# Second feed-forward product as seven half products, operands in the attentions' buffers

## Chip, core and metric

The kernel runs on one core of a Trainium2 chip. The metric is the device time of one execution in microseconds (us). Three executions were timed and one more was profiled.

## What is computed

Three layers follow each other, for a batch of 4 sequences of 448 positions and 768 channels:

```python
# 1: causal attention, 12 heads of 64
x = softmax(causal(q @ k.T / 8)) @ v
# 2: four one-head attentions (experts) on x; each position takes its best two
logits = x @ w_gate
out = sum(gate[e] * (softmax(causal((x @ wq[e]) @ (x @ wk[e]).T / 8)) @ (x @ wv[e])) @ wo[e] for e in range(4))
# 3: feed-forward with a gate from a convolution over positions (3 taps)
h = relu(out @ w_in)                      # 768 -> 1024
y = h * sigmoid(conv(h, conv_w))
result = y @ w_out                        # 1024 -> 768: the product that is changed
```

`w_in`, `conv_w` and `w_out` arrive as 64-bit floats.

## The kernel before

Every product is made from numbers split in two: a high part (`hi`) that TensorE takes without loss, and the rest (`lo`). Three matmuls (`PASSES`) stand for one exact product: hi by hi, hi by lo, lo by hi. Splitting a tile therefore takes two elementwise instructions, a copy for hi and a subtraction for lo. ScalarE is called ACT, VectorE DVE, GpSimd POOL and SyncE SP, as in the profile.

**Stages.** For each batch `b` there are six attention jobs of two heads (`A`, from layer 1), the projections of layer 2 (`proj_qk`, `proj_v`) and two jobs of layer 2's attentions (`M`). Layer 2's `wo` and layer 3's `w_in` are folded into one matrix `wp` beforehand (`fold_all`). `ffn_batch` makes, for each batch, eight chunks of 128 feed-forward channels: six matmuls with 448 moving columns (L1188), then relu, convolution, tanh, the gate product (L1219), and the split of the result `g` (L1223, L1226). `ffn_out(b, n)` makes 128 output channels of a batch: for each of the eight chunks three matmuls of 448 moving columns against `wout` (L1251), 24 in all, then one copy out of PSUM and one store of 224 KB.

**Weights.** `wout_convert` takes `w_out` in 12 pieces of 512 columns: a load, a conversion from 64-bit floats (one ACT and four DVE instructions, `from_f64`), hi on ACT (L1105), lo on POOL (L1108), and a store into device memory. When the attentions of layer 1 are over, six loads of 1 MB bring the split weights back (`wout_load`).

**Order.** Nothing is scheduled at run time. All tasks are numbered as they are added, and `ORDER` is a packed list, written out beforehand by a planner, which gives the order of the tasks and, where a task may run on several engines (`either`), the engine. Each engine executes its tasks in that order. The planner's costs are in the code; for a matmul it reckons

```python
def mm(n, k=1):
    return k * max(n / 2.2, 96.0)
```

**Buffers.** Tiles come from rings (`RINGS`), PSUM banks from `BANKS`. The operands `g` of two batches have room at once: eight tiles in a pool of their own and eight in the ring of `xT`. The rings `P` and `PT` hold the attentions' probabilities and their transposes, `skM` the operands of layer 2's attentions. The part of the order behind layer 1's last attention mixes the projections and the `M` jobs of batch 3 with `ffn_batch` and `ffn_out` of batches 0 to 2: `M[3, 0]` ends its product with the values before the first `ffn_out` of batch 0 is over, `M[3, 1]` in the midst of batch 1's.

Of the kernel before, what the change touches and what calls it, by code (L numbers as in the profile page):

```python
# [14 lines left out]
I64 = mybir.dt.int64  # L15
# [25 lines left out]
    "ST9h^C~Li|-e3QWv&q@z9CD60Z#k!|e^Dqjh~B6#*GKEQa-E!pHpw|?pFArM%P&w@s2^Al*dI9Ooc(%rr?zuI{-GX1!)Q~dqZ5*QJ0G*2vOd>8"
    "WA)eN>OQcpS?Ic?+%AXZg}SA>mAd!!=k>SsC^=XsuDj%fJCmJyv>9zjU)IBQ)H*De$YpRj+_}2%YwmU4aE9gMb@@78-I)BD{E_^L{IUE&rxz{b"
    "66E7GlQlCng_`*q6<5!-a7#6dHLEpLxsR)>8|UUbr|M$pFn79hwsW*|uJilO&6=$mXWed1r6yA6sq5$FxjF7Ecc{)-w@|lHx6pZ5b5e6zb6Qib"
    "JFY9q*W|Y~0F^)mcyub4Dxqf4IW)){Mh|h5bxH1`e2NQGljtIs%Y%3@Z%h8NQ^)i2LcDGH7<vM2;vv*Y+H>wS?Fns-wn5vWEphEUD(_?6`?^nc"
    "=XIBLW~!6wqeiG{YCrW)-T*blyRAd93G7e2$LIq3Gw*^oOdX>>qEgv!xo@~1Xg{MD&<|?X<=fmT>Qn0L&L#9JI?LNYm(deEGkuVrr#tAsb?$WT"
    "bq>?#X>Vx*ylwPz+Ck?pEG}Ej{-*vJ^#!#eSFj`W6>f!l!hK17MSa`3NIRen@lx~+>T%~4cb~g2@1q~f&$u_-hrEyIL-Z8=wDTX{9S_4N@@IJS"
    "yeB+t7p-f7hwtL@mw78Zi2siIp1Mc<MCEiHQ+0e3|Cn|`{Yt~o?`Rjaubn=AmJf9)y2AWl1dD=K0+?UnAMoAWP2MP7+hyku@RR&u{utjwpQY#d"
    "fPf<q3qZje!4>tEN}$u|0F6MS)3`J-jVkyXUF6Tvm*@)G?}BZCrRyo5OIOkn`Z@oSe=gt(A>pL}5n2Hq%}jIBe6$EnOoxSK-Vy(ruMi-D9bTH&"
    "N6XRv?PT)b&|lGC(6{In`U!oTzE3};8-;)n6jFtk=o|E7eu=-v-{4;h973-U4V<F?7J$G<!6!jUxFp;ZmW3X{B7cj&&A*~w(_Mn7z#>Qs`UHc5"
    "A;GvHFQ^F5g#VR)m2V5b6W$YMgi+y$a8x)cEC`Fj8#$)oK<MuB0%70*jliHW%#1LD3akiuz!#x|kpkEZJCFrt1f&K=1Fzvocq2rM7$TxbDv~f1"  # L50
    "3=cyBz`%cKTZ|pXA!Ay2#Q>Q%j3<IQ0b7)0Xc<{Xj&aNw5siy<4W<TP1C?oS2sbE2W|2dLh<qX};|E|;ByBiv0ALWlZ1})H02K3-!C^wokf^^Q"
    "*YJ>WpYfRSh*4ma7&D?k*KhD&@H_ZDJOv~hij1KKDm)9!0bCe@#~RY2KGAakfpelIV4`8VVE|ZU!0;NQAo>Uc3Y`K}Y%s1H=0yu4lVY}ENyJs?"
    "nJ%V^X<_=9X=WcY%p7D6Gw%cAz-RaZ{tB-&EH+RTp{`<sT>&XzMXD>?mFpVr@+ww<apnZm2!|A#igU%K!U4Z%*lc*)uqLV~b{h^G-T<4TEzz#X"
    "3*UpwiXW9vlmqa!Vov!&nSm>!L(vxS2ar-^6%Q5L3bgV-@uA_k;Yfj3<`j<<N1`(kP03N}l@(<O9)TxeKwN;&mFk9{x_(u@Qod1MD#u`j@<2%t"
    "11h>0RB^=;u~KXjBjSHVYR$j!6g=AXsB1`3gg*c?ig`r|ey2PDmK9RvF~Cus0ha((wV-&SxCR#CRamUDD4oim)&Gi$T?7eDVwQv@UZq14&|ol5"
    "u}>Tkr^Wr^LGhUQNO`SPs1Vh#_{S~+hKkve>_|RH4kgDDql$ykYb+X<CZg<D=9H7-s3xlNtDbkIlrySX)r`0xo)?$I%i<03ieg3VQl(XWszKG2"
    "WL!0&I+bKJ_cTjgt6dviZ@b=ifl{jUMuL+5)wQYG67PyD;zRL?_+0!&TvpwP(NIaX2}vXz=~>sF>at5Ax#>FUl6lY`B1DCFkQ7ouddLDfAdiGC"
    "(MtT#k}3+NpnFgb8dBjsBg#=_Qj(SAB=@1b<i2D?Gp2#0d8JFb1?@r=NG~0SN}46j_nL>28O^?GMFo4lQE#h?s$<n-iArjbPC_$K0h)(qHAT&t"
    "3ZpJa`qU-KqGU}1sy8GXnxdoxEkdi1vI%K=t2u<6P2Q#zjZYeqrlohP2~Ad-Zpt<pn|3sV(qZXv(^nN;Em3pS3iS!}o%$5IufBvz>P>a1NvAfd"
    "|LpohInXrP^dI#j^<(u@^`7Qbv!q^8SJVgUGxZmBS-q{!Hyx=FkICckOgAkw{m5Kw8kaiN9(B5LS6k8Mr8jDHBfhcNlx_5SW*TQ3i;d44!|IX7"  # L60
    "vBpoD&zi5ATMfF2&_rwcrTJy^tL8V&1C29UZWGj0(9Ub0HZeT^LIvrvbWXY|r8Z79vKtp0R~y%wwwl(PcAB=N2htts2Wh2A+Nf+aH`*JIqz_sj"
    "wmxdzXxwi+Xu?W-vVK`umXj?=*QMIVaoMaaFPoD28pDkx?Rhh|1!*z1oJlXGPz&5LB)e?BZU$Pw7HZ4;#*dBf8c!Op8h>wo-+b11(+Frzn$DU&"
    "HZx?OnoBK9Et@Te+7oS2mXzT&&t*$8q6{OulX7KZnNo(xDlKO%<(7k%?UpYsW|>_^*F0|BY&~yvw0K)&m}JXJ%Vkr@^Gfzc_Fh(&aWs&I@9Aqn"
    "8!NIC*_G@@b|$N|E^F7c=h|q?z6_|(cz$Yq*7~A#pyg%jQOixsWoucxp)I$fTN$kftykI`EgHcaVa!O&WD5bIBO^vGB0-dh4*4E4gmIg`H6fVk"
# [53 lines left out]
class Program:  # L118
# [146 lines left out]
def attn_moe_ffn_kernel(  # L265
# [352 lines left out]
    def head(j, h, moe):  # L618
# [87 lines left out]
        for i in range(NQ - 1, -1, -1):  # L706
# [4 lines left out]
            elif i:  # L711
# [5 lines left out]
                if not first:  # L717
                    first = j.taken = [t]
# [666 lines left out]
```

## Time and profile before

| | |
|---|---|
| median of three executions | 503.1 us (501.62 to 504.71) |
| profiled execution, its own time | 503.03 us |
| its span in the trace | 501.2 us |
| granted TensorE clock, mean | 0.996 |
| TensorE busy (matmuls) | 487.5 us |
| DVE, ACT, POOL busy | 369.0, 349.8, 261.9 us |

The span runs from the first instruction to the last; 1.8 us of the profiled time lie around it. A matmul's busy time includes its way through the array, and matmuls overlap, so that TensorE shows as busy also across short gaps. What one matmul costs in a row of many is the time of the row divided by their number.

### The profile page before, as it was taken

To read this page: it belongs to the slowest core of one execution; us is meant where nothing else is said; L and a number is where in the kernel's file an instruction comes from. 1 tells how busy PE (TensorE), PEld (TensorE's weight loads), DVE (VectorE), ACT (ScalarE), POOL (GpSimd) and SP (SyncE) were. 2 spreads that over 40 slices of the span, in tenths; PEclk is the share of its full clock that TensorE was granted. 3 is DMA by queue.
4 is the path that set the end of the run, shared out by engine and by line. 5 is a ranking of instruction groups with operands and counts; after the bars stand their busy time and mean duration, and the time that the engine had idled before them with its cause. 6 is when DMAs were issued, how large, how long until landed. Compare 5 with 4: busy or idle time off the path is not lost.

```text
span 501.2 us, 9905 instructions
## 1 busy us (share of the span) xinstructions
PE 487.5 (97%) x3202; PEld 419.7 (84%) x3202; DVE 369.0 (74%) x1110; ACT 349.8 (70%) x970; POOL 261.9 (52%) x388
## 2 busy tenths in 40 slices
PE   8788999999999999999999999999999999999997
PEld 6656878988888898888988788898999989999996
DVE  4999999988899686987789984487587556374300
ACT  5989999998889768886888893386566554344201
POOL 1856879978879777998788944162022002000000
PEclk9999999999999999999999999999999999999999
DMA  8857468996793767665688615838220112101011
GB/s 216 211 164 186 128 179 225 232 250 192 203 242 106 178 173 214 142 176 136 202 204 237 151 57 168 272 148 213 88 90 0 56 37 80 51 16 58 37 38 73
DMA packets 29171, 73.03 MB, mean 146 GB/s; under 512 B 4160, under 2 KB 11072, under 8 KB 28352
## 3 DMA queue, kind: packets, MB, share of 16 engines
q1 hardware_dynamic: 29040, 72.18, 51.8%
q8 instruction: 25, 0.41, 0.4%
q10 hardware_dynamic: 80, 0.23, 0.2%
q14 instruction: 26, 0.21, 0.1%
HBM read 50.50 MB, written 13.63 MB: 128 GB/s over the span
## 4 chain that ended last, share of the span: by engine, by line
PE 74%; DVE 11%; POOL 5%; DMA 4%; issue 2%; ACT 1%; SPq 0%; POOLq 0%; DVEq 0%; ACTq 0%
PE bank L1251 23%; PE bank L952 9%; PE bank L690 9%; PE bank L760 9%; PE bank L637 9%; PE bank L1188 8%; PE bank L998 4%; DMA nat<-in_qk_dram 4%; DVE P_A L650 3%; PE bank L881 3%; POOL sk_A L340 2%; DVE PT_A L337 1%; POOL P_M L333 1%; POOL P_A L333 1%; DMA cwraw<-in_conv_w_dram 1%
## 5 line engine op out<-in xcount | busy, mean ns | idle before, releaser
L1251 PE MATMUL bank<-g,wout 128*128 128x448 f32 x576 | 123.2, 367 | 0.0
L1251 PEld LDWEIGHTS bank<-g,wout 128*128 128x128 f32 x576 | 107.4, 188 | 8.8
L659 ACT ACTIVATE P_A<-P_A,nm_A 112x448 f32<-112x448 f32 (+3 forms) x192 | 99.4, 521 | 15.7 <-DVE nm_A L650 10.4
L340 POOL TENSOR_TENSOR sk_A<-nat,sk_A 64x448 fp32r<-64x448 f32 (+1 forms) x77 | 90.3, 1172 | 9.7 <-ACT sk_A L331 3.9
L650 DVE CUSTOM_DVE_ANT_0 P_A<-bank,mask 112x448 f32<-112x448 f32 (+3 forms) x192 | 80.0, 440 | 10.8 <-PE bank L595 6.3
L637 PE MATMUL bank<-sk_A 128*112 128x112 f32 (+3 forms) x352 | 66.4, 312 | 3.5 <-DVE nm_A L650 2.9
L952 PE MATMUL bank<-xT,wqk 128*128 128x448 f32 x288 | 68.7, 374 | 0.6 <-DVE sk_M L968 0.4
L690 PE MATMUL bank<-ident,P_A 112*112 112x112 f32 x480 | 61.7, 264 | 3.3 <-DVE xT L792 1.4
L333 POOL TENSOR_SCALAR P_A<-P_A,r_A 112x336 f32<-112x336 f32 (+3 forms) x97 | 49.9, 526 | 25.7 <-DVE r_A L670 9.2
L637 PEld LDWEIGHTS bank<-sk_A 128*112 128x112 f32 x352 | 48.8, 176 | 10.1 <-DVE nm_A L650 4.5
L690 PEld LDWEIGHTS bank<-ident,P_A 112*112 112x112 f32 x480 | 49.8, 135 | 8.0 <-DVE xT L792 1.6
L952 PEld LDWEIGHTS bank<-xT,wqk 128*128 128x128 f32 x288 | 51.2, 188 | 4.1 <-DVE sk_M L968 0.5
L1209 DVE SCALAR_TENSOR_TENSOR bank<-h,cw,bank 128x448 f32<-128x448 f32 x64 | 43.5, 687 | 14.8 <-ACT bank L1207 11.6
L760 PE MATMUL bank<-PT_A,v 112*64 112x448 f32 (+3 forms) x384 | 50.4, 406 | 0.1
L760 PEld LDWEIGHTS bank<-PT_A,v 112*64 112x64 f32 x384 | 26.2, 137 | 23.6 <-issue 12.3
L331 ACT ACTIVATE P_A<-P_A,r_A 112x448 f32<-112x448 f32 (+3 forms) x87 | 42.3, 517 | 4.6 <-DVE r_A L670 4.3
L1188 PE MATMUL bank<-ocs,wp 128*128 128x448 f32 x192 | 43.5, 367 | 0.0
L998 PE MATMUL bank<-wvg,xT 128*112 128x260 f32 x288 | 41.2, 287 | 0.2 <-DVE wm L434 0.2
L333 POOL TENSOR_SCALAR sk_A<-nat 128x896 fp32r<-128x896 f32 x35 | 33.0, 941 | 12.6 <-DMA nat<-in_qk_dram 11.6
L1188 PEld LDWEIGHTS bank<-ocs,wp 128*128 128x128 f32 x192 | 35.7, 188 | 3.0
L659 ACT ACTIVATE P_M<-P_M,nm_M 112x224 f32<-112x224 f32 (+3 forms) x64 | 33.3, 522 | 6.8 <-DVE nm_M L650 5.3
L331 ACT ACTIVATE PT_A<-bank 112x336 f32<-112x336 f32 (+1 forms) x75 | 33.9, 472 | 5.2 <-PE bank L690 5.0
(105 smaller groups left out, 820.2 us busy)
## 6 DMA issues: line engine op xcount, KB each, us to landing
nat<-in_qk_dram SPq DMA_DIRECT2D x88, 224.0 KB, 4.0
wraw<-in_w_in_dram SPq DMA_DIRECT2D x12, 512.0 KB, 5.5
woraw<-in_w_out_dram SPq DMA_DIRECT2D x12, 512.0 KB, 5.1
wo<-wohl SPq DMA_DIRECT2D x12, 512.0 KB, 4.1
wout<-wo SPq DMA_DIRECT2D x6, 1024.0 KB, 10.0
v<-in_v_dram SPq DMA_DIRECT2D x24, 224.0 KB, 4.5
out_dram<-osb SPq DMA_DIRECT2D x24, 224.0 KB, 1.9
sk_M<-sk_M SPq DMA_DIRECT2D x16, 224.0 KB, 4.2
```

Source lines behind the costliest of these rows:

```text
L331: nc.scalar.activation(dst, src, AF.Copy, scale=scale)
L333: nc.gpsimd.tensor_scalar(dst, src, scale, 1.0 if scale2 is None else scale2, ALU.mult, ALU.mult)
L340: (nc.gpsimd if e == "POOL" else nc.vector).tensor_tensor(dst, a, b, op)
L637: nc.tensor.matmul(sp[:CP], t[:, j.o[h], m * CP : (m + 1) * CP], t[:, j.o[h] + k, :w], start=(k == 2), stop=(k == 1),)
L650: nc.vector.tensor_tensor_reduce(rows(i), st["s", i][:CP, :w], mask[:, S - w :], -SCALE, 3.0e38, ALU.add, ALU.min, st["nm"][:, i : i + 1],)
L659: nc.scalar.activation(rows(i), rows(i), AF.Exp, bias=st["nm"][:, i : i + 1], scale=-1.0, accum_out=st["sm"][:, i, 0:1],)
L690: nc.tensor.transpose(pt[:CP, o : o + CP], rows(i)[:, kt * CP : (kt + 1) * CP], ident[:CP, :CP])
L760: nc.tensor.matmul(st["ov"][h * D : (h + 1) * D, kt * CP : S], j.v[:, kt, h, :], j.PT[h][:, col_base[kt] : col_base[kt] + S - kt * CP], st ...
L952: nc.tensor.matmul(st["ps"][:, :S], proj["wqk"][:, a, cc, w, p * P : (p + 1) * P], xT[b, cc][:, b2, :], start=(cc == 0 and (a, b2) == PASS ...
L998: nc.tensor.matmul(st[i][:CP, :VW], xT[b, cc][:, a, i * CP : (i + 1) * CP], proj["wvg"][:, b2, cc, :], start=(cc == 0 and (a, b2) == PASSE ...
L1188: nc.tensor.matmul(st["ps", c][:, :S], wp[:, a, ec, c * P : (c + 1) * P], st["oc", ec][:, b2], start=(ec == 0 and (a, b2) == PASSES[0]), s ...
L1251: nc.tensor.matmul(st["ps"][:, :S], ffn["wout", n][:, a, c], gs[c][:, b2], start=(c == 0 and (a, b2) == PASSES[0]), stop=(c == NFC - 1 and ...
```

## The change

`ffn_out(b)` computes a batch's product of 768 by 1024 and 1024 by 448 as a two by two block product with seven multiplications in place of eight (Strassen's scheme in Winograd's form). The weight blocks are 384 by 512, the operand blocks 512 by 224. So there are seven products (`PRODUCTS`), each of three groups of 128 rows (`HO`), each of four chunks (`HC`), each of three passes: 252 matmuls of 224 moving columns a batch in place of 144 of 448.

- Four sums of weight blocks are needed. `wout_convert(m, q)` now converts blocks in pairs and adds and subtracts them (24 instructions of 256 columns), splits seven blocks in place of four, and stores 24 pieces, 10.5 MB in place of 6 MB (`wset_d`, in runs of 1 KB). Seven loads of 1.5 MB bring the sets back.
- Four sums of operand blocks are needed. `chunk_pair` makes, of two chunks, three sums (`t13`, `t2`, `t4`) and splits seven blocks, in four pieces. `mul` writes its result into SBUF in place of PSUM; the factor 0.5 has moved into relu.
- The seven products are summed up in `ffn_sum`, eight instructions of 224 columns for each group of rows, 96 in all, in place of 24 copies of 448. The stores are 32, of one or two quarter blocks.
- The pool `g` is gone. `unit_space` lends out 22 tiles of the rings `xT`, `skM`, `vm`, `PT` and `P`, when the attentions are through with them: 4 for `g` and the sums (`w`), 18 for split operands (`u`). A batch needs 14 of the 18, and 2 for its input.
- `ORDER` is new. Read out against the numbering of the tasks, it differs in this: before layer 1's attentions are over, POOL has 8 copies and 7 subtractions of `q` and `k` less and 3 scalings of probabilities more; ACT has 6 of the copies, 15 evictions of transposes and 4 scalings more; DVE has 7 of the subtractions and 2 of the copies more, 15 evictions and 7 scalings less. Of the weights' copies to hi, 7 are on ACT and 17 on DVE (12 on ACT before), of their subtractions 16 on POOL and 8 on DVE (12 on POOL before), of their sums 20 on POOL and 4 on DVE. Of the operands' sums 27 are on POOL and 21 on DVE, of their splits' copies 31 on ACT, 18 on POOL, 15 on DVE, and of their subtractions 38 on POOL and 26 on DVE. The 24 pieces of converted weights are 6 of 256 columns and 18 of 512. Of the operands' 16 pairs of chunks each has one sum of 448 columns (9 on POOL, 7 on DVE) and two of 224, three splits of 448 columns (17 subtractions and 11 copies on DVE) and one of 224. Both `M` jobs of batch 3 now come directly behind that batch's projections, and end before the second product of batch 0 is well begun; eight `ffn_batch` chunks stand between their steps.

```diff
-    BANKS = dict(s=(0, 1, 4), t=(2, 3, 5), v=(4, 5), m=(6, 7), h=(6, 7, 0, 2), o=(5, 3, 1))
+    BANKS = dict(
+        s=(0, 1, 4), t=(2, 3, 5), v=(4, 5), m=(6, 7), h=(6, 7, 0, 2), o=(5, 3, 1, 4),
+        w=(102, 103, 104, 105), u=(100, 101, *range(106, 122)),
+    )
...
+    PRODUCTS = ((0, "b11"), (1, "b21"), (2, "t2"), (4, "t3"), (5, "t1"), (3, "b22"), (6, "t4"))
...
+        a22 = parts(lambda: vals[1]()[:, 1:2], 1, 6, [vals[1, "t"]])
+        s1 = combine(at(1, 1), at(1, 0), at(1, 1), ALU.add, a22)
+        up = parts(lambda: vals[0](), 2, 0, [vals[0, "t"]])
+        s3 = combine(at(1, 0), at(0, 0), at(1, 0), ALU.subtract, s1 + [vals[0, "t"]])
+        parts(lambda: vals[1](), 2, 4, s3, wms[1:])
+        s2 = combine(at(0, 0), at(1, 1), at(0, 0), ALU.subtract, s3 + up)
+        s4 = combine(at(0, 1), at(0, 1), at(0, 0), ALU.subtract, s2)
+        parts(lambda: vals[0](), 2, 2, s4, wms[:1])
...
+        give([10, 11, 12], of_sk, [t for j in M.values() for t in j.taken], [Buf("skM")])
+        give([13], of_vm, [t for j in M.values() for t in j.vready], [Buf("vm")])
...
+            t = give([14 + k], of_pt, [j.first_tr for j in every] + [t], [Buf("PT")])
...
-                nc.vector.scalar_tensor_tensor(y, y, 1.0, st[c][:, 1 : S + 1], ALU.add, ALU.mult)
+                nc.vector.scalar_tensor_tensor(
+                    g()[:, k], st["ps", c][:, :S], 1.0, st[c][:, 1 : S + 1], ALU.add, ALU.mult
+                )
...
+        t = [add(either("tadd", b, of_two(S)), 0, t13, muls, take=[tb], free=[gb])]
+        t13_done = t
+        t = [add(either("tadd", b, of_two(HS)), 0, t2, t, free=[gb])]
+        t24_done = [add(either("tadd", b, of_two(HS)), 0, t4, t, free=[gb])]
...
+            th = add(either("ghi", b, of_one(n)), 0, hi, dep + after, take=take, free=[buf])
+            tl = add(either("glo", b, of_two(n)), 0, lo, [th], free=[buf])
...
-                    nc.tensor.matmul(
-                        st["ps"][:, :S],
-                        ffn["wout", n][:, a, c],
-                        gs[c][:, b2],
-                        start=(c == 0 and (a, b2) == PASSES[0]),
-                        stop=(c == NFC - 1 and (a, b2) == PASSES[2]),
...
+                            nc.tensor.matmul(
+                                ps(pb)[:, :HS],
+                                wset[s][:, a, m, c2 * P : (c2 + 1) * P],
+                                u[:, b2, o : o + HS],
+                                start=(c2 == 0 and (a, b2) == PASSES[0]),
+                                stop=(c2 == HC - 1 and (a, b2) == PASSES[2]),
+                            )
...
+    SUMS = (
+        (("s", None),),
+        (("c11", "s"),),
+        (("u", "s"),),
+        (("s", "u"),),
+        (("c22", "s"), ("u", "u")),
+        (("c12", "u"),),
+        (("c21", "s"),),
+    )
...
+            if src:
+                nc.vector.tensor_tensor(w, acc, st[src, m], ALU.add)
+            else:
+                copy(e, w, acc)
...
+    for n, (s, _) in enumerate(PRODUCTS):
+        wset_load(s, [ta] if n < 4 else [tg], "wa" if n < 4 else "wb")
     for b in range(B):
-        ffn_batch(b, cwt, [ta, tg] if b % 2 else [ta])
+        ffn_batch(b, cwt, [ta])
     for b in range(B):
-        for n in range(NCC):
-            ffn_out(b, n)
+        ffn_out(b)
```

## Rows read from the trace of the kernel before

**Rows 1.** The page, busy time, share of the span and instructions by engine.

```profile
PE 487.5 (97%) x3202; PEld 419.7 (84%) x3202; DVE 369.0 (74%) x1110; ACT 349.8 (70%) x970; POOL 261.9 (52%) x388
```

**Rows 2.** Busy time in three stretches: PE, PEld, DVE, ACT, POOL, clock, DMA, GB/s.

```profile
50.00:100.00 50.00, 49.45 (x382) 41.65 (x383) 48.76 (x166) 47.72 (x145) 43.12 (x52) 1.00 0.73 190
100.00:300.00 200.00, 198.28 (x1490) 169.22 (x1489) 172.20 (x589) 167.16 (x500) 161.79 (x222) 1.00 0.67 180
350.00:450.00 100.00, 100.00 (x518) 90.52 (x515) 60.87 (x115) 54.20 (x112) 10.90 (x33) 1.00 0.16 52
```

**Rows 3.** Chain that ended last, shares by line, of 75 to 300 and 300 to 502.

```profile
by line: PE bank L690 16.3%; PE bank L637 15.9%; PE bank L952 14.7%; PE bank L760 14.4%; PE bank L881 7.0%; PE bank L998 5.7%; POOL sk_A L340 4.5%; DMA nat<-in_qk_dram 3.3%; POOL P_M L333 2.8%; issue 2.3%; POOL P_A L333 1.8%; DVE P_A L650 1
...
by line: PE bank L1251 58.2%; PE bank L1188 19.4%; PE bank L952 5.7%; PE bank L760 5.0%; PE bank L998 4.4%; PE bank L690 2.9%; PE bank L637 2.2%; ACT osb L331 0.3%; issue 0.0%; ACTq L331 0.0%
```

**Rows 4.** The same chain in order of time: start, length, what, number.

```profile
107.53 1.44 PE bank L881 x12
...
319.76 1.22 PE bank L1188 x6
...
411.14 2.04 PE bank L760 x16
...
461.70 35.88 PE bank L1251 x177
```

**Rows 5.** Groups by line and form: the changed product, weight loads of 128 and 112 columns.

```profile
L1251 PE MATMUL bank<-g,wout 128*128 128x448 f32 x576 | 123.2, 367 | 0.0
L1251 PEld LDWEIGHTS bank<-g,wout 128*128 128x128 f32 x576 | 107.4, 188 | 8.8
...
L637 PEld LDWEIGHTS bank<-sk_A 128*112 128x112 f32 x352 | 48.8, 176 | 10.1 <-DVE nm_A L650 4.5 <-DVE xT L792 0.7 <-issue 0.3
```

**Rows 6.** Timeline of weight loads, windows at 8.4, 6.5 and 77.9: start, length, number.

```profile
8.18 0.52 PEld L1320 LDWEIGHTS bank<-ident 128*128 128x128 f32 x4 [0.48 <-issue]
...
6.52 0.30 PEld L1320 LDWEIGHTS bank<-ident 128*128 128x128 f32 x2 [0.67 <-issue]
...
77.84 0.28 PEld L637 LDWEIGHTS bank<-sk_A 128*112 128x112 f32 x2
```

**Rows 7.** Groups by line and form: elementwise work like what is added or moved.

```profile
L1108 POOL TENSOR_TENSOR wohl<-wm,wohl 128x512 fp32r<-128x512 f32 x12 | 15.4, 1289 | 3.4 <-ACT wohl L1105 2.4 <-POOL sk_A L340 0.9
...
L1105 ACT ACTIVATE wohl<-wm 128x512 fp32r<-128x512 f32 x12 | 7.5, 625 | 2.3 <-DVE wm L434 2.3
...
L340 POOL TENSOR_TENSOR sk_A<-nat,sk_A 64x448 fp32r<-64x448 f32 x42 | 50.0, 1191 | 5.4 <-ACT sk_A L331 1.4 <-POOL P_A L333 0.8
...
L333 POOL TENSOR_SCALAR sk_A<-nat 128x896 fp32r<-128x896 f32 x35 | 33.0, 941 | 12.6 <-DMA nat<-in_qk_dram 11.6 <-PE bank L637 0.6
...
L331 ACT ACTIVATE sk_A<-nat 128x896 fp32r<-128x896 f32 x9 | 8.5, 948 | 0.5 <-DMA nat<-in_qk_dram 0.5
...
L331 ACT ACTIVATE PT_A<-bank 112x336 f32<-112x336 f32 x52 | 22.7, 443 | 3.9 <-PE bank L690 3.9
...
L340 DVE TENSOR_TENSOR sk_A<-nat,sk_A 64x448 fp32r<-64x448 f32 x2 | 1.2, 622 | 0.1
...
L340 DVE TENSOR_TENSOR sk_A<-nat,sk_A 128x448 fp32r<-128x448 f32 x9 | 7.7, 851 | 0.7 <-ACT sk_A L331 0.7
...
L1209 DVE SCALAR_TENSOR_TENSOR bank<-h,cw,bank 128x448 f32<-128x448 f32 x64 | 43.5, 687 | 14.8 <-ACT bank L1207 11.6 <-POOL ocs L1163 1.9 <-issue 0.5
...
L1219 DVE SCALAR_TENSOR_TENSOR bank<-bank,h 128x448 f32<-128x448 f32 x32 | 19.9, 628 | 7.9 <-ACT bank L1215 7.6
...
L650 DVE CUSTOM_DVE_ANT_0 P_A<-bank,mask 112x224 f32<-112x224 f32 x48 | 18.2, 382 | 0.8 <-PE bank L595 0.5
```

**Rows 8.** DMA issues: number, KB each, median us from issue to landing.

```profile
wo<-wohl SPq DMA_DIRECT2D x12, 512.0 KB, 4.1
...
wout<-wo SPq DMA_DIRECT2D x6, 1024.0 KB, 10.0
```

More of the change, by code (lines that the diff above doesn't have):

```diff
@@ L1 @@
 from contextlib import ExitStack
+from functools import partial
 import base64
@@ L393, in attn_moe_ffn_kernel, with from_f64 @@
     open_pool("w", "right")
-    def from_f64(raw, raw_buf, load, shape, n, need=(), take=()):
+    def from_f64(raw, raw_buf, load, shape, n, need=(), take=(), own=None):
         st = {}
@@ L434, in flush @@
             nc.vector.scalar_tensor_tensor(m, m, 2.0**-30, view(st["ps"]), ALU.is_ge, ALU.mult)
-        ts = add("ACT", act_sb(n) + 35, square, [load], take=[sq], free=[raw_buf])
-        t = add("DVE", dve(n), bits, [load, *need], take=[mb, *take])
+        ts = add("ACT", act_sb(n) + 35, square, [load, *need], take=own[0] if own else [sq], free=[raw_buf])
+        t = add("DVE", dve(n), bits, [ts], take=[mb, *take])
         t = add("DVE", dve(n), top, [t])
@@ L446, in mk @@
         j.kind, j.b, j.p = kind, b, p
+        j.began = []
         return j
@@ L1180, in ffn_batch, with chunk_pair, g, tt @@
-        for c in range(NFC):
+        his[b] = []
+        for c2 in range(HC):
+            chunk_pair(b, c2, cwt, need, st, obs, oc, od)
+    def chunk_pair(b, c2, cwt, need, st, obs, oc, od):
+        gb, tb = Buf("w"), Buf("w")
+        def g():
+            return unit(gb)
+        def tt():
+            return unit(tb).rearrange("p a (k n) -> p (a k) n", k=2)
+        muls = []
+        earlier = pairs[-2] if len(pairs) > 1 else []
+        for k in range(2):
+            c = c2 + HC * k
@@ new lines, in chunk_pair, with t13, t2, t4 @@
+            muls.append(add("DVE", dve(S), mul, [t] + muls + earlier, take=[] if k else [gb], free=[hb, mb]))
+        def t13(e):
+            both = g().rearrange("p a n -> p (a n)")[:, :S].rearrange("p (a n) -> p a n", a=2)
+            two(e, tt()[:, 0:2], g()[:, :, HS:], both, ALU.subtract)
+        def t2(e):
+            two(e, tt()[:, 2], g()[:, 1, HS:], tt()[:, 0], ALU.subtract)
+        def t4(e):
+            two(e, tt()[:, 3], g()[:, 1, :HS], tt()[:, 2], ALU.subtract)
+        t = [add(either("tadd", b, of_two(S)), 0, t13, muls, take=[tb], free=[gb])]
@@ new lines, in ffn_out, with part, go @@
+    def ffn_out(b):
+        st = {}
+        tmp = {(k, m): Buf("tmp") for k in ("s", "u") for m in range(HO)}
+        obuf = {}
+        for step, (s, name) in enumerate(PRODUCTS):
+            for m in range(HO):
+                pb = Buf("o")
+                t = None
+                def part(c2, s=s, name=name, m=m, pb=pb):
+                    def go():
+                        ub, o, _ = operands[b, c2, name]
+                        u = unit(ub)
+                        for a, b2 in PASSES:
+                            nc.tensor.matmul(
[4 more added lines that the diff above has]
+                                stop=(c2 == HC - 1 and (a, b2) == PASSES[2]),
+                            )
+                    return go
+                for c2 in range(HC):
+                    ub, _, dep = operands[b, c2, name]
+                    t = add(
+                        "PE", mm(HS, 3), part(c2), dep + wset_done[s] + [t],
+                        take=[] if c2 else [pb], free=[ub],
+                    )
+                for dst, src in SUMS[step]:
+                    ffn_sum(b, m, st, tmp, obuf, t, pb, dst, src)
```

454 lines of the change are left out of this document (285 added, 169 removed).

## The prediction

> **What bounds the kernel now.** I read the page first, then the stretches, then the chain in shares, then the chain in order of time, and last the groups of the changed lines. The page shows TensorE busy 97% of the span and every other engine at 74% or less [rows 1]. Busy is a share of overlapping matmuls, so the chain decides. It splits the run in two. From 75 to 300 us matmuls have 74% of the chain; a fifth lies on POOL, DVE and ACT, 3.3% on a wait for a load [rows 3]. There those three are busy 162 to 172 of 200 us [rows 2]: a stage in which TensorE leads, with little room beside it. From 300 us on the matmul lines have 98% of the chain, L1251 alone 58% [rows 3], while DVE and ACT are busy 61 and 54 of 100 us and POOL 11 [rows 2]. So the change takes matmul time from the stage that consists of it, puts splitting work into the half-empty engines beside it, and weight sums into the full stage ahead.
>
> **The change, part by part.** The working is against the profiled execution, 503.03 us, which is the median of 503.1 within 0.1; its span is 501.2.
>
> *The product itself.* Before: 35.88 us for 177 matmuls in a row [rows 4] is 0.2027 us for 448 columns, and 576 of them [rows 5] cost 116.8 us, all on the chain. After: 7 products x 3 groups x 4 chunks x 3 passes x 4 batches are 1008 matmuls of 224 columns. The planner prices one at 224 / 2.2, or 0.102 us. No row shows 128 stationary columns with 224 moving ones. What streaming would cost follows from two rows: half of 0.2027 is 0.101, and 1.44 us for 12 matmuls of 256 columns [rows 4], 0.120 each, scaled to 224 gives 0.105; I take 0.103. But each matmul brings its own weight load, 576 for 576 [rows 5]. A load of 128 columns lasts 0.188 us and one of 112 lasts 0.176 [rows 5], so part of it goes with the columns. Four loads of 128 columns in a row take 0.52 us; less the 0.19 of the last one, three steps take 0.33, which is 0.110 each [rows 6]. The pair that begins a burst shows the same, 0.30 less 0.19 [rows 6], and a pair of 112 columns about 0.10 [rows 6]. With 448 columns such a load hides behind the streaming (0.110 under 0.203), with 256 as well (under 0.120); with 224 it doesn't (0.110 over 0.103). I take 0.110 as nearest, since it is the step of just this load: 1008 x 0.110 = 110.9, a gain of 5.9 us, where the planner's price would give 14.0. The ends are 0.101 (101.8, a gain of 15.0) and the row of 256 columns, 0.120 (121.0, a loss of 4.2).
>
> The Trainium skill says in TensorE: Matmul & The Clock Gate, section LDWEIGHTS (loading the stationary operand), that a load takes its columns divided by 1.2 ns, however many rows it has. That speaks against halves: 106.7 ns for 128 columns, by which the product would cost 107.6 us, a gain of 9.2. The step in the rows is 3 ns longer, and I stay with the rows. The same page, section Back-to-back issue gap, gives columns / 2.4 + 2.5 ns for one matmul behind another, 95.8 ns for 224 columns, an estimated 96.6 us and a gain of 20.2; for 448 it gives 189.2, and the trace, with 202.7, doesn't agree.
>
> *Weight sums and the new order, ahead of 300 us.* The conversions from 64 bits stay (12 pieces). Priced by rows 7, with 256 columns at half of 512 and a scaling like an eviction: POOL loses 8 copies (0.94) and 7 subtractions (1.19), gains 3 scalings (0.44), and has 11 subtractions of 512 columns (1.29) and 25 subtractions or sums of 256 (0.6) for 12 of 512: +0.5 us. ACT gains 6 copies (0.95), 15 evictions (0.44), 4 scalings, and loses 3.7 us of weight copies (0.62): +10.4. DVE gains 7 subtractions (0.62), 2 copies, 8 weight subtractions (0.85 for 448 columns), 17 weight copies, which no row shows (0.3 to 0.6 for 512, I take 0.5), and 4 sums, and loses 15 evictions and 7 scalings: +13.4. That is 24 us on three engines. They are busy 501 of 3 x 200 us [rows 2], hence 564 in 75 to 300, and have at most 20.4% of that chain, 46 us [rows 3]: of each microsecond of their work, 8% lies on the chain. 24 x 8% is 2.0 us. The ends are -3, since the re-dealt order may take some of POOL's 4.5% (10 us) off the chain, and +13.4, if all that DVE gains lands on it; I stay low since ACT and DVE are at 84% and 86% [rows 2] and are given 5 and 6 points more. SP issues 24 saves for 12, 4.5 MB more, 11% of the 40 MB moved at 180 GB/s in 225 us [rows 2]; 11% of the 7.4 us that the chain waits for loads is 0.8.
>
> *The last attentions, the buffers and the operands, behind 300 us.* Before, the product with the values of the last job stands at 411 us amid second products [rows 4]. Now the rings must be empty before most of the 18 tiles can be lent, so both jobs run early, covered by the projections and eight chunks. Summing the matmuls of the new order at the paces of the rows, 6 to 7 us of them lie between a head's last score and its first transpose, where the old order had 12 to 29. `mul`, the sums, both halves of the splits and the quarter sums lie beside matmuls: per batch DVE has 16 x 0.687 + 8 x 0.628 for convolution and gate, 22.5 x 0.382 for quarter sums, and by the dearer SBUF row (0.85, halves 0.43) 3.0 for operand sums, 4.6 for subtractions, 2.0 for copies: 34 us, against 8 x 1.22 + 252 x 0.110 = 37.5 of matmuls [rows 4, 7]. DVE just fits; it was at 61%. From a chunk's matmuls to the first product that reads it the order keeps at least 8 us of matmuls, 17 beyond batch 0; the chain through relu, convolution, gate and split needs some 6. The seven weight loads of 1.5 MB should take 15 us at the pace of 1 MB in 10.0 [rows 8], and sets 3 and 6 are issued 15 us ahead of their first use. If a cover fails, those 30 us of last attentions behave like the stage before, a quarter off the matmuls [rows 3]: 8 us. The ends are 0 (as now, 98%) and 8; I take 2.0, as the covers are thin in one place only. The last sum and store are smaller than the last copy and store now; I count nothing.
>
> Sum: 503.0 - 5.9 + 2.0 + 0.8 + 2.0 = 501.9 us.
>
> **Rivals.**
> - *Streaming sets the pace.* If the next load can begin while an earlier matmul still waits for its own weights, 224 columns cost 0.103: 103.8 us, a gain of 13.0, and 503.0 - 13.0 + 4.8 = 494.8 us. For it: the planner's price, and the unbroken proportion from 448 to 256 columns. Against it: the steps in rows 6. The skill's gap rule above points the same way.
> - *The weight sums fill the stage ahead.* Place: 75 to 300 us, on DVE. Before 100 us DVE is busy 98% and ACT 95% [rows 2]; if the new work brings DVE there up to 300 us too, each added microsecond lies on the chain. It decides once DVE is above about 95%; my count brings it to 92%. Price 13.4 in place of 2.0: 513.3 us, slower.
> - *Half the columns isn't half the time.* If a matmul with its load stays at the 0.120 us of 256 columns, the product costs 121.0 in place of 116.8, and seven products do no less than eight: 503.0 + 4.2 + 4.8 = 512.0 us.
>
> **How the numbers follow.** A measurement of this kernel can tell about 1% (5 us) from no change. Forecast 60%, with 497 to 508 as its own range (gain 5.9, costs from 0 to 11); streaming 17%; weight sums 17%; no shorter 6%. Faster by over 1% (below 498): 16% from streaming and 12% from forecasts with hardly any cost, 28%. Slower (above 508): 15 from the weight sums, 5 from the last rival, 2 from the forecast, 22%. Within 1%: 50%. The range of 494 to 512 leaves out 6% below and 12% above.
>
> **What would show it.** The forecast's main step: L1251's successor in a long row at 0.110 us a matmul, and weight loads that follow each other without idle time; 0.103 with idle time between loads would be the first rival. The second: between 75 and 300 us a matmul share of the chain well under 74%, DVE over 95% busy, the last layer 1 attention later by 10 us. For the last attentions: idle TensorE between 300 and 350 us, ended by DVE or POOL on `P_M`, or by a weight load. Behind that, the chain should stay at 95% or more on matmuls. The prediction fails by most if the start moves: up to 100 us DVE is nearly full [rows 2], and the order is new there too.

## The result, and the profile after

The changed kernel takes 505.4 us (median of 20 executions, 502.76 to 508.37) against 501.63 of the kernel before, run beside it (20 executions, 499.96 to 504.96): a ratio of 1.0065, interval 1.0043 to 1.0086, 3.3 us slower (the ratio goes by all the executions; the two medians alone differ by 3.8 us). The prediction said 1.1 us faster, in a range that holds the result. The profiled execution took 504.77 us, with a span of 502.9.

First the page of the changed kernel, its line of busy times.

```profile
PE 488.5 (97%) x3664; PEld 427.2 (85%) x3664; DVE 414.0 (82%) x1235; ACT 353.9 (70%) x982; POOL 343.5 (68%) x483
```

Against [rows 1], DVE has 45 us more, POOL 82 and ACT 4; TensorE's busy time says as little as before. The groups of the new product's line, one of its five operand pools:

```profile
L1444 PE MATMUL bank<-ux,ws 128*128 128x224 f32 x360 | 53.5, 275 | 0.0
...
L1444 PEld LDWEIGHTS bank<-ux,ws 128*128 128x128 f32 x360 | 47.2, 192 | 0.5
```

The weight loads follow each other with 0.5 us of idle time for 360, where the old product's had 8.8 for 576 [rows 5]. The chain gives the pace; the shares by line of 75 to 300 us and of 300 to the end, each with one of its longest pieces, then pieces of the last attentions:

```profile
by line: PE bank L656 13.4%; PE bank L780 13.4%; PE bank L709 13.2%; PE bank L1018 9.9%; PE bank L972 9.4%; PE bank L901 3.9%; DMA sk_M<-sk_M 3.3%; issue 3.1%; DMA wset<-wohl 3.1%; DVE P_A L669 3.0%; POOL sk_A L353 2.6%; POOL P_A L346 2.3%;
...
154.76 3.18 DVE P_A L350
...
by line: PE bank L1444 55.5%; PE bank L1331 17.8%; PE bank L972 7.2%; PE bank L780 4.9%; PE bank L1018 4.4%; PE bank L709 2.1%; PE bank L656 1.8%; DVE bank L1352 1.3%; DVE ux L1361 0.5%; DVE P_M L669 0.5%; ACT P_M L678 0.5%; DVE PT_M L350 0
...
453.22 46.23 PE bank L1444 x414
...
343.23 0.69 DVE bank L1352
...
344.88 0.55 DVE ux L1361
...
345.47 1.47 PE bank L1331 x6
```

46.23 us for 414 matmuls is 0.1117 each. Between 75 and 300 us the matmul lines shown have 63% where they had 74 [rows 3], and one DVE step alone has 3.18 us. (Such a share sets no price: in run 5 below the same lines have 57%, and that kernel is the faster one.) The step is an attention scaling of 112 columns. The timeline around it, DVE, POOL and TensorE (start, length, what; in brackets the idle time ahead and its releaser):

```profile
153.47 0.18 DVE L689 RECIPROCAL r_A<-r_A 112x4 f32<-112x4 f32 x1
...
154.68 3.27 DVE L350 TENSOR_SCALAR P_A<-P_A,r_A 112x112 f32<-112x112 f32 x1
157.87 0.49 DVE L669 CUSTOM_DVE_ANT_0 P_A<-bank,mask 112x336 f32<-112x336 f32 x1
...
169.37 0.40 DVE L350 TENSOR_SCALAR P_A<-P_A,r_A 112x336 f32<-112x336 f32 x1
...
153.82 0.82 POOL L346 TENSOR_SCALAR P_A<-P_A,r_A 112x336 f32<-112x336 f32 x1 [0.28 <-DVE r_A L689]
154.61 0.94 POOL L346 TENSOR_SCALAR sk_A<-nat 128x896 fp32r<-128x896 f32 x1
155.52 1.26 POOL L892 TENSOR_TENSOR whl<-wm,whl 128x512 fp32r<-128x512 f32 x1
156.74 2.35 POOL L353 TENSOR_TENSOR sk_A<-nat,sk_A 128x448 fp32r<-128x448 f32 x2
...
154.79 1.12 PE L709 MATMUL bank<-ident,P_M 112*112 112x112 f32 x10
158.42 0.61 PE L656 MATMUL bank<-sk_A 128*112 128x224 f32 x4 [2.51 <-DVE nm_A L669]
...
159.64 3.60 PE L780 MATMUL bank<-PT_A,v 112*64 112x448 f32 x16
...
340.91 1.74 PE L1571 MATMUL bank<-ident 128*128 128x128 f32 x14
342.83 1.30 PE L656 MATMUL bank<-sk_M 128*112 128x448 f32 x8 [0.18 <-DMA sk_M<-sk_M]
...
344.66 0.62 PE L1571 MATMUL bank<-ident 128*128 128x128 f32 x4
345.47 1.47 PE L1331 MATMUL bank<-ux,wp 128*128 128x448 f32 x6 [0.18 <-DVE ux L1361]
```

(L1571 are matmuls on the identity that only keep TensorE busy.) A scaling three times as wide took 0.40 us at 169.37. This one took 3.27, while POOL worked without a break from 153.82 to 159.1. Its reciprocal was there at 153.65. Behind it on DVE's queue stood a row maximum, for which TensorE's next scores waited 2.51 us. The windows show what that left (columns as in [rows 2]):

```profile
0.00:75.00 75.00, 68.97 (x482) 52.94 (x483) 65.65 (x235) 67.19 (x202) 55.14 (x73) 1.00 0.74 202
...
75.00:300.00 225.00, 220.47 (x1649) 186.17 (x1649) 207.33 (x674) 196.65 (x581) 184.50 (x248) 0.99 0.74 200
...
156.00:159.00 3.00, 0.58 (x5) 0.58 (x6) 3.00 (x5) 0.32 (x1) 2.92 (x3) 1.00 0.78 269
159.00:162.00 3.00, 3.00 (x14) 1.31 (x15) 2.86 (x8) 2.38 (x6) 0.09 (x1) 0.68 0.11 36
162.00:165.00 3.00, 3.00 (x24) 1.77 (x22) 2.93 (x10) 2.92 (x9) 1.15 (x1) 0.75 0.83 255
165.00:168.00 3.00, 3.00 (x29) 2.76 (x26) 2.11 (x6) 2.60 (x9) 2.70 (x3) 1.00 0.93 221
```

After the idle stretch the granted clock is 0.68 and 0.75 for 3 us each, so part of them ran at the lower level, 1.2 GHz: 3 x 0.32 + 3 x 0.25 is 1.7 us of lost clock. With the gap of 2.5 us that is about 4.2 us, more than the whole loss of 3.3.

### The profile page after: what moved, and what is told of

Its sections match the earlier page's. It is cut to its first block, busy times and chain, and to the rows that moved or that the text cites. A ratio compares the mean times of both kernels' runs of the same rounds, so it can differ in the third digit from the quotient of the medians.

```text
span 502.9 us, 11134 instructions
## 1 busy us (share of the span) xinstructions
PE 488.5 (97%) x3664; PEld 427.2 (85%) x3664; DVE 414.0 (82%) x1235; ACT 353.9 (70%) x982; POOL 343.5 (68%) x483
## 4 chain that ended last, share of the span: by engine, by line
PE 69%; DVE 14%; DMA 6%; POOL 5%; issue 2%; ACT 2%; SPq 1%; DVEq 0%; POOLq 0%; ACTq 0%
PE bank L1444 22%; PE bank L780 9%; PE bank L656 8%; PE bank L972 8%; PE bank L709 7%; PE bank L1331 7%; PE bank L1018 6%; DVE P_A L669 4%; PE bank L901 2%; DMA nat<-in_qk_dram 2%; POOL P_A L346 2%; POOL sk_A L353 2%; DMA sk_M<-sk_M 1%; DMA wset<-wohl 1%; DVE PT_A L350 1%
## 5 line engine op out<-in xcount | busy, mean ns | idle before, releaser
L678 ACT ACTIVATE P_A<-P_A,nm_A 112x112 f32<-112x112 f32 (+3 forms) x192 | 99.8, 523 | 13.5 <-DVE nm_A L669 12.8
L353 POOL TENSOR_TENSOR sk_A<-nat,sk_A 128x448 fp32r<-128x448 f32 (+1 forms) x70 | 81.9, 1171 | 10.5 <-ACT sk_A L344 6.2
L346 POOL TENSOR_SCALAR P_A<-P_A,r_A 112x448 f32<-112x448 f32 (+3 forms) x96 | 53.6, 570 | 16.2 <-DVE r_A L689 6.5
L1444 PE MATMUL bank<-ux,ws 128*128 128x224 f32 x360 | 53.5, 275 | 0.0
L1444 PEld LDWEIGHTS bank<-ux,ws 128*128 128x128 f32 x360 | 47.2, 192 | 0.5
L344 ACT ACTIVATE P_A<-P_A,r_A 112x112 f32<-112x112 f32 (+3 forms) x91 | 44.0, 513 | 2.5 <-DVE r_A L689 2.4
L678 ACT ACTIVATION_READ_ACCUMULATOR P_A<-P_A,nm_A 112x1 f32 x192 | 37.2, 194 | 0.0
L1018 PEld LDWEIGHTS bank<-wvg,xT 128*112 128x112 f32 x288 | 36.5, 175 | 0.6
L1358 ACT ACTIVATE bank<-bank 128x448 f32<-128x448 f32 x32 | 16.7, 524 | 28.6 <-DVE bank L1352 28.5
L346 POOL TENSOR_SCALAR P_M<-P_M,r_M,g_w 112x112 f32<-112x112 f32 (+3 forms) x59 | 33.9, 588 | 4.0 <-PE bank L709 2.4
```

What stands on the lines that cost most here:

```text
L344: nc.scalar.activation(dst, src, AF.Copy, scale=scale)
L346: nc.gpsimd.tensor_scalar(dst, src, scale, 1.0 if scale2 is None else scale2, ALU.mult, ALU.mult)
L353: (nc.gpsimd if e == "POOL" else nc.vector).tensor_tensor(dst, a, b, op)
L678: nc.scalar.activation(rows(i), rows(i), AF.Exp, bias=st["nm"][:, i : i + 1], scale=-1.0, accum_out=st["sm"][:, i, 0:1],)
L1018: nc.tensor.matmul(st[i][:CP, :VW], xT[b, cc][:, a, i * CP : (i + 1) * CP], proj["wvg"][:, b2, cc, :], start=(cc == 0 and (a, b2) == PASSE ...
L1444: nc.tensor.matmul(ps(pb)[:, :HS], wset[s][:, a, m, c2 * P : (c2 + 1) * P], u[:, b2, o : o + HS], start=(c2 == 0 and (a, b2) == PASSES[0]) ...
```

## The experiments

Ratios are to the kernel before, run on the same chip in the same session (its medians there were 501.1 to 502.5 us). Where several executions were timed, the interval follows. The edits are shown abridged.

**1. The old product with each matmul cut in two halves.**

```diff
-nc.tensor.matmul(st["ps"][:, :S], ffn["wout", n][:, a, c], gs[c][:, b2], ...)
+for x in range(0, S, S // 2):
+    nc.tensor.matmul(st["ps"][:, x : x + S // 2], ffn["wout", n][:, a, c], gs[c][:, b2, x : x + S // 2], ...)
```

> The kernel before, with each matmul of 448 moving columns in the second product split in two of 224: 1152 in place of 576, all else as it was. Weight loads set the pace: 0.112 us each, as in the trace of the changed kernel, 129.0 us in place of 116.8, so 12.2 us slower, a ratio of about 1.024 to the kernel before. Streaming sets the pace: 0.102 each, 117.5 us, a ratio of 1.001.

Measured: 1.0231 (1.0199 to 1.0263), 11.6 us more. The longest row of the product in its chain:

```profile
468.95 39.53 PE bank L1252 x354
```

0.1117 us again, in a kernel in which nothing else is changed: 1152 x 0.1117 - 116.8 is 11.9 us.

**2. Stationary columns 112 in place of 128**, in 11 of 12 matmuls of the changed kernel's product.

```diff
-ps(pb)[:, :HS], wset[s][:, a, m, c2 * P : (c2 + 1) * P], u[:, b2, o : o + HS],
+ps(pb)[:cp, :HS], wset[s][:, a, m, c2 * P : c2 * P + cp], u[:, b2, o : o + HS],   # cp = 112
```

> The changed kernel, with 112 of 128 stationary columns in 11 of 12 matmuls of each group of the second product, so that most of the last 16 output channels of each group of 128 are left out. Weight loads set the pace: a load of 112 columns takes about 0.098 us, streaming 224 columns 0.102 to 0.104 then binds, 924 matmuls gain 0.008 each, 7.4 us, a ratio of about 0.992 to the kernel before where the changed kernel has 1.0065. Streaming sets the pace: no change, 1.0065. Something else between matmuls of different products (issue, PSUM): no change either.

**3. Moving columns 192 in place of 224**, in the same matmuls.

```diff
-u[:, b2, o : o + HS],
+u[:, b2, o : o + 192],
```

> The changed kernel, with 192 of 224 moving columns in 11 of 12 matmuls of each group of the second product, so that most of the last 32 positions of each half are left out. Weight loads set the pace: no change, 0.110 to 0.112 us a matmul and a ratio of 1.0065. Streaming sets the pace: 32 columns less are 0.0145 us less for 924 matmuls, 13.4 us, a ratio of 0.980.

Measured: 0.9903 (0.9872 to 0.9934) with fewer stationary columns, 1.006 (1.003 to 1.009) with fewer moving ones. The longest rows, first of 2, then of 3:

```profile
448.85 43.16 PE bank L1445 x414
```

```profile
454.32 46.22 PE bank L1445 x414
```

0.1043 and 0.1116 us. A seventh of the moving columns taken away changes nothing, an eighth of the stationary ones takes 7 ns. The weight load sets the pace of this product. With 112 columns the streaming does: take the one matmul in twelve at 0.1117 out of 0.1043, and 0.1036 is left, inside the prediction's 0.101 to 0.105 for streaming, while loads of 112 columns can follow each other faster. Transposes with 112 stationary and 112 moving columns run at 0.096 in the chain of the kernel before (0.96 us for 10, at 70.65).

**4. The slow scaling on ACT**, the one step of the list moved.

```diff
-prog.run(steps_of(ORDER), warm)
+prog.run([(n, "ACT" if n == 1328 else e) for n, e in steps_of(ORDER)], warm)
```

> The changed kernel, with one scaling of 112 columns of probabilities moved from DVE to ACT: the one that takes 3.27 us at 154.7 us in the trace, while POOL runs without a break. First theory, that this stall costs TensorE 2.7 us of idle time and some 1.7 us of half clock behind it: 4.4 us less, a ratio of about 0.998, and no dip of the granted clock at 160 us. Second theory, that DVE and POOL keep each other from SBUF so often that the stall moves to the next copy on DVE: no change, 1.0065.

Measured: 0.9975 (0.995 to 1.0001), 500.81 us, 4.5 us less than the changed kernel. Its timeline, the row maximum that had waited, then TensorE, then a second place:

```profile
154.72 0.50 DVE L669 CUSTOM_DVE_ANT_0 P_A<-bank,mask 112x336 f32<-112x336 f32 x1
...
155.70 0.59 PE L656 MATMUL bank<-sk_A 128*112 128x224 f32 x4
...
189.27 2.99 DVE L350 TENSOR_SCALAR wohl<-wom 128x256 fp32r<-128x256 f32 x1
...
188.74 2.26 POOL L346 TENSOR_SCALAR P_M<-P_M,r_M,g_w 112x112 f32<-112x112 f32 x4
190.97 1.14 POOL L353 TENSOR_TENSOR sk_A<-nat,sk_A 128x448 fp32r<-128x448 f32 x1
...
192.50 1.15 PE L656 MATMUL bank<-sk_A 128*112 128x336 f32 x6 [1.14 <-DVE nm_A L669]
```

The gap at 156 us is gone. At 189 us, however, a weight copy of 256 columns is held for 2.99 us. The first move does not bring this on: in runs 2 and 3, whose kernels differ from the changed one only behind 300 us, the same copy was held for 2.99 us as well. In the changed kernel's profile it took 0.29 us, although POOL's row went on there too:

```profile
193.67 0.29 DVE L350 TENSOR_SCALAR wohl<-wom 128x256 fp32r<-128x256 f32 x1
...
193.63 0.67 POOL L346 TENSOR_SCALAR P_M<-P_M,r_M,g_w 112x224 f32<-112x224 f32 x1
```

It came just as one POOL step ended (at 193.65) and the next began, and that next step took 0.67 us, where the same one took 0.54 in run 3. So it seems that a few hundredths of a microsecond decide, from one execution to the next, whether this copy is held. Both held steps go from SBUF to SBUF, and both end with a POOL subtraction of `sk_A`.

**5. That copy on ACT as well.**

```diff
-prog.run(steps_of(ORDER), warm)
+prog.run([(n, "ACT" if n in (1328, 2313) else e) for n, e in steps_of(ORDER)], warm)
```

> The changed kernel with two of its steps moved from DVE to ACT: the attention scaling that took 3.27 us at 154.7 us, and the weight copy that took 2.99 us at 189.3 us in the run with only the first one moved (the same copy took 0.29 us in the profiled run of the changed kernel). Theory: a DVE step that goes from SBUF to SBUF waits while POOL runs without a break, and what is queued behind it on DVE waits as well; with both steps gone the second gap in TensorE, 1.3 us, goes too. That gives about 1 us less than with one step moved, a ratio of 0.995 to 0.997. Rival: the gain of the first move was luck of the order, and any further move costs ACT, at 84 to 90 percent in that stage, as much as it gives: 0.998 to 1.002.

Measured: 0.9958 (0.9937 to 0.998), faster than both kernels. Against run 4 the intervals overlap; the span of the profiled execution is 0.5 us shorter.

**6. One step out of POOL's row**, the scaling left on DVE.

```diff
-prog.run(steps_of(ORDER), warm)
+prog.run([(n, "ACT" if n == 1250 else e) for n, e in steps_of(ORDER)], warm)   # 1250: POOL's scaling of sk_A
```

> The changed kernel with one POOL step, the scaling of a query half right ahead of the slow DVE scaling, moved to ACT; the slow scaling itself stays on DVE. Theory: DVE's scaling waits for POOL's unbroken row, so with 0.94 us taken out of that row it lasts about 2.3 us in place of 3.27, and the gap of TensorE behind it shrinks from 2.5 to about 1.6 us. Rival: the scaling is slow for a reason of its own (its operands, a wait that the profile books on it); then it still lasts about 3.3 us.

A single execution: 500.93 us, span 499.1; as a time it says little (the kernel before took 499.98 to 505.85 us beside it), so the trace has to tell. DVE, POOL, TensorE:

```profile
154.12 1.28 DVE L350 TENSOR_SCALAR P_A<-P_A,r_A 112x112 f32<-112x112 f32 x1
...
154.06 1.27 POOL L892 TENSOR_TENSOR whl<-wm,whl 128x512 fp32r<-128x512 f32 x1
156.34 2.38 POOL L353 TENSOR_TENSOR sk_A<-nat,sk_A 128x448 fp32r<-128x448 f32 x2 [1.01 <-ACT sk_A L344]
...
155.88 0.61 PE L656 MATMUL bank<-sk_A 128*112 128x224 f32 x4 [0.53 <-DVE nm_A L669]
```

More than expected: POOL now waits 1.01 us for ACT behind its subtraction, and the scaling ends with that subtraction, after 1.28 us. Same scaling, same engine: POOL's row is what held it.

**7. The same with the copy of run 5 on ACT.**

```diff
-prog.run(steps_of(ORDER), warm)
+prog.run([(n, "ACT" if n in (1250, 2313) else e) for n, e in steps_of(ORDER)], warm)
```

> The changed kernel with POOL's scaling of the query half and the weight copy at 189 us on ACT, the slow attention scaling left on DVE. Theory (what counts is whether POOL's row breaks, not where the scaling runs): as fast as with the scaling itself moved, a ratio of 0.994 to 0.998, and no gap of TensorE over 1.2 us between 75 and 300 us. Rival: the single run without rounds was a chance, and the slow scaling keeps costing some 3 us with it: 1.000 to 1.006.

Measured: 0.9994 (0.9969 to 1.0019), 500.84 us. The interval lies across both expectations and decides nothing between them; against the changed kernel's 1.0065 it is 0.0071 less, 3.6 us, and those two intervals do not overlap. In the trace the scaling takes 1.27 us and TensorE's gap behind it 0.56; but one of 1.25 us stands at 247.7, where scores wait for a transfer (`sk_M`), and the theory had allowed none over 1.2. Run 4 has 1.23 us at the same place, so this gap is not the edit's doing.

**8. Without the added weight work**, the scaling on ACT.

```diff
-return [add(either("wadd", 0, of_two(FW)), 0, lambda e: two(e, dst(), a(), b2(), op), need)]
+return [add(either("wadd", 0, of_two(FW)), 0, lambda e: None, need)]
...
+if s0 in (4, 6): return          # in hi, lo and save
+if s > 3: wset[s] = wset[s - 4]; return   # in load
```

> The changed kernel with the slow scaling on ACT, and without the 24 weight sums and the splits, saves and loads of the last three weight sets; the products that would read those sets read the first three. So it leaves out all weight work that the change adds, and the time is the price of that work. Theory of the prediction, that 8 percent of each added microsecond lies on the chain and the saves cost 0.8 us: 2 to 3 us less than with the scaling moved alone (0.9975), a ratio of 0.991 to 0.994. Rival, the weight work fills the stage: 8 us or more less, 0.982 or below. Second rival, the re-dealt order hides it all: no difference, 0.996 to 0.999.

Measured: 0.9901 (0.9866 to 0.9935), 497.65 us. That is a little below the 0.991 to 0.994 expected, which was reckoned from run 4. Beside run 5, which was timed in the same session and has no held copy either, this is 0.0057 less, 2.9 us, give or take some 2. The first theory holds; both rivals are out.

**9. The same, the scaling back on DVE.**

```diff
-prog.run([(n, "ACT" if n == 1328 else e) for n, e in steps_of(ORDER)], warm)
+prog.run(steps_of(ORDER), warm)
```

> The kernel without the weight sums and the splits, saves and loads of the last three sets (its products read the first three), but with the attention scaling left on DVE as in the changed kernel. Ahead of that scaling DVE then lacks the copy (0.41 us) and the subtraction (0.66 us) of a weight set, which stood behind the reciprocal that the scaling needs. Theory: these two steps pushed the scaling behind the start of POOL's unbroken row; without them it starts before or with that row, lasts under 1.5 us, and the kernel is as fast as with the scaling on ACT, a ratio of 0.987 to 0.993. Rival: the new order alone makes the stall, since none of POOL's steps in that row is a weight sum; then the scaling still takes about 3 us and the ratio is 0.996 to 1.002.

Measured: 1.0032 (1.0004 to 1.006), 502.69 us: nearer the rival's 0.996 to 1.002, and a little above it. The one step costs 0.013 in the ratios, and 3.9 us in the spans (500.8 against 496.9). DVE, POOL, TensorE:

```profile
152.91 3.55 DVE L350 TENSOR_SCALAR P_A<-P_A,r_A 112x112 f32<-112x112 f32 x1
...
152.61 0.54 POOL L346 TENSOR_SCALAR P_A<-P_A,r_A 112x336 f32<-112x336 f32 x1 [0.70 <-DVE r_A L689]
153.12 0.95 POOL L346 TENSOR_SCALAR sk_A<-nat 128x896 fp32r<-128x896 f32 x1
154.03 1.27 POOL L892 TENSOR_TENSOR whl<-wm,whl 128x512 fp32r<-128x512 f32 x1
155.25 2.35 POOL L353 TENSOR_TENSOR sk_A<-nat,sk_A 128x448 fp32r<-128x448 f32 x2
...
156.94 0.61 PE L656 MATMUL bank<-sk_A 128*112 128x224 f32 x4 [2.24 <-DVE nm_A L669]
```

My theory falls: with no weight step ahead of it the scaling starts 1.8 us earlier and is held 3.55 us by the same row. The weight work doesn't make the stall. The order does: the step stood on POOL in the old list and stands on DVE in the new one, beside a full row of POOL.

**10. Without the third tap of the convolution in batch 0**, the scaling on ACT.

```diff
-else:
+elif b or j < 2:
     nc.vector.scalar_tensor_tensor(y, h, w, y, ALU.mult, ALU.add)
```

> The changed kernel with the slow scaling on ACT, and without the third tap of the convolution in the first batch (8 DVE steps of 0.69 us, which stand beside the last attentions). Theory: between 304 and 353 us TensorE loses 3.1 us more than in the kernel before (idle time and matmuls on the identity that only fill), because ACT and DVE, convolution first, are late there; with 5.5 us of DVE work gone 1 to 3 us come back, a ratio of 0.992 to 0.996. Rival: the order of the matmuls alone makes the gap, DVE has room there (28 of 50 us), and nothing changes: 0.997 to 0.999.

**11. Without the fill at 337 and 341 us**, scaling and copy on ACT.

```diff
-if r is not None and n > 0:
+if r is not None and n > 0 and since < 3e5:
```

> The changed kernel with the scaling and the copy on ACT, and without the 18 matmuls on the identity (2.1 us) that only fill TensorE in front of the second score and in front of the second half of a chunk, at 337 and 341 us. Theory: the scores wait for the last keys and queries (a transfer of 3.87 us behind their split, seen once the third taps were left out) and the chunk waits for the gate's multiplication, so TensorE stands idle where it filled, and the time stays that of the kernel with both steps on ACT, a ratio of 0.994 to 0.998. Rival: the fill itself is the cost; then 1.5 to 2 us come back, 0.991 to 0.993.

**12. Without fill and tap**: the edits of runs 10 and 11 together.

> The same without the fill and also without the third tap of the convolution in the first batch (8 DVE steps). Theory: the scores at 338 us are still released by the transfer of the keys and queries, so from the last scores of layer 1 to the first second product it takes 47.5 to 48.5 us, where the kernel with the fill and without the taps took 48.3. Rival: fill and taps each hid the other; with both gone it falls by 2 us or more, to 46 us.

Measured: 0.9961 (0.9936 to 0.9986) without the tap, 0.999 (0.9965 to 1.0015) without the fill, 499.99 us in a single execution without both. The first ratio lies at the edge of its theory, the second above both of its expectations, though its interval overlaps that of run 5. The traces decide: from the end of layer 1's last product with the values to the first second product it takes 48.3 us in run 4, 48.1 without the tap, 48.3 without the fill, 48.1 without both. So neither was the cost. The timeline of run 11:

```profile
337.58 1.30 PE L656 MATMUL bank<-sk_M 128*112 128x448 f32 x8 [1.73 <-DMA sk_M<-sk_M]
...
340.24 1.49 PE L1331 MATMUL bank<-ux,wp 128*128 128x448 f32 x6 [0.67 <-DVE ux L1361]
```

Where the fill was, TensorE now waits 1.73 us for the transfer that brings the last keys and queries, and 0.67 for the gate product.

## Why the prediction was wrong

**The product (-5.9): right mechanism, size off.** The weight load sets the pace, as runs 1 to 3 show, and the rival of the streaming falls; so does that of the 0.120 us, which reckoned the product at 121.0. But a step is 0.1117 us, not 0.110: 1008 x 0.1117 is 112.6, a gain of 4.2, 1.7 us less. The four loads of [rows 6] that gave 0.110 are a burst with an idle start; a row of some hundreds was the thing to know, and the kernel before has none. The gap rule that the prediction takes from the Trainium skill (TensorE: Matmul & The Clock Gate, section Back-to-back issue gap) is there the gap of an isolated matmul; of a stream of loads and matmuls the section says that both set the spacing, and in runs 1 to 3 the load does.

**The weight sums and the new order (+2.0, and 0.8 for the saves): the step that failed.** For the work itself it was good: 2.9 us, give or take 2, in run 8 for 2.8, and DVE at 92% of 75 to 300 us as counted, so that the rival of the full stage (over 95%) never came. Of that rival's signs only the lower matmul share of the chain did. What failed is "of each microsecond of their work, 8% lies on the chain". A mean share prices each added microsecond alike and each moved step at its length. The new order moved one scaling from POOL to DVE, 0.3 to 0.4 us by the rows of its like, and it cost 4.5 us (run 4): held 3.27 us beside POOL's unbroken row, with the row maximum behind it, TensorE's scores behind that, and the half clock behind those (runs 4, 6 and 9). My bounds of -3 and +13.4 held the sum, but no part of the working named a DVE step that waits for POOL, and no rival did.

The Trainium skill has this in SBUF — State Buffer, section Who interferes with whom: DVE and GpSimd share a pair of ports, a `tensor_scalar` between SBUF tiles can be one of those that want it, and whoever issues first has it for its whole instruction while the other blocks fully. I hadn't weighed it. Run 6 agrees, 1.28 us up to the end of one subtraction. The changed kernel and run 9 don't: there DVE waited through three and four POOL instructions in a row (3.27 and 3.55 us). Why it waited for one there and for more here, no run shows.

The trace of the kernel before had the sign already. There, too, a DVE scaling of 112 columns lasted until a POOL subtraction ended, at 100.7 us; no scores stood behind it:

```profile
99.77 1.04 DVE L337 TENSOR_SCALAR P_A<-P_A,r_A 112x112 f32<-112x112 f32 x1
...
99.45 1.29 POOL L1108 TENSOR_TENSOR wohl<-wm,wohl 128x512 fp32r<-128x512 f32 x1
```

**The last attentions (+2.0): right size, as far as the trace tells.** The place that [rows 2, 3] couldn't show costs 1.74 + 0.62 us of fill and 0.18 + 0.18 of idle time, 2.7 us; no run took these waits away. The reason given was half right. That the covers are thin is so (runs 11 and 12), but the late ones are the transfer of the last keys and queries and the chain through convolution and gate together; DVE's load was not it, nor was a wait on `P_M` or for a weight load, the signs that the prediction named. The chain behind 300 us has some 94% on matmuls, not 95 or more. Weight loads and the tail cost nothing that shows, as reckoned.

**The sum.** With the product at -4.2, 2.9, 2.7 and 4.5 it would be +5.9; measured is +3.3. No run was made for the rest, -2.6 us, but the traces say where it lies. Layer 1's last product with the values stands at the same place before and after, and 6.0 us earlier in run 8, which has neither the stall nor the added weight work:

```profile
300.29 3.99 PE L760 MATMUL bank<-PT_A,v 112*64 112x448 f32 x32
...
300.25 3.99 PE L780 MATMUL bank<-PT_A,v 112*64 112x448 f32 x32
...
294.24 3.99 PE L780 MATMUL bank<-PT_A,v 112*64 112x448 f32 x32
```

Behind it, however, the new order has 72 projection matmuls of 448 columns in place of 54, work of 18 x 0.2027 = 3.6 us that it has put off. So in the profiled executions, which differ by 1.7 us in all, the part ahead lost 3.6 us, where 2.9 + 4.5 would be 7.4, and the part behind gained 1.9, near the 1.5 of -4.2 + 2.7. In run 8 the part ahead is 6.0 - 3.6 = 2.4 us shorter than before. That is what the re-dealt order itself gains there, as far as single executions tell; the prediction had it as the lower end of a range (-3) and at nothing in the sum. The start, counted at nothing too, is within it: up to 75 us TensorE is busy 68.97 us in place of 66.65, though 1.6 us of that are 12 more filling matmuls. Run 4, the change without its stall, is 0.25% faster than before (its interval reaches no change), where the forecast for the change was 0.2%; that its errors cancel so well is partly luck.

## What to carry to other kernels

Before a re-dealt order is priced by averages, look for single steps that change between DVE and POOL, and read in the timeline what the other engine does without a break beside them and who stands behind the step; here a step of 0.3 to 0.4 us cost 4.5. A DVE scaling that takes longer than its like beside POOL, as one did in the kernel before, is the warning. A product with few moving columns costs its weight loads: cut the moving columns by half and only what exceeds the load's step is gained (here 0.2027 us became twice 0.1117). And moving one step to a third engine is a cheap repair, here worth more than the change itself.

## What the runs showed of the hardware

- A DVE scaling or copy from SBUF to SBUF was held for 1.0 to 3.6 us beside POOL, up to some ten times its length, while row maxima from PSUM (0.49 us) ran at their usual pace beside the same POOL steps. It got its turn at the end of one POOL instruction (run 6, and 99.77 us in the kernel before) or only after three or four.
- 128 stationary columns with 224 or 192 moving ones step at 0.1117 us in long rows. The Trainium skill (TensorE: Matmul & The Clock Gate, section LDWEIGHTS) gives 106.7 ns for the load; the trace has 5 ns more.
- An idle stretch of 2.5 us was followed by 6 us at a mean granted clock of 0.72; in run 6, with 0.53 us idle at the same place, it stayed at 1.00.
